# A third buffer for transposed q and k, a slot of lead for the heads' preparation, fewer score and half buffers

## The chip, the cores and the metric

The kernel runs on one core of one Trainium2 chip. The metric is the device time of one execution in microseconds (us). Engines are PE (TensorE, with its weight loads as PEld), DVE (VectorE), ACT (ScalarE), POOL (GpSimd) and SP (SyncE, which here only issues DMAs).

## The reference

Three layers follow each other on 4 x 576 = 2304 tokens, all in float32: causal attention with a decay (8 heads of 64), a gated two-branch layer, and a mixture of eight experts in which each token goes to one.

```python
scores = scale * np.matmul(q, k.transpose(0, 1, 3, 2))
cum = np.cumsum(np.log(np.clip(f, 0.0001, 1.0)), axis=-1)
scores = np.where(causal, -1000000000.0, scores + cum[:, :, :, None] - cum[:, :, None, :])
attn = np.exp(scores - scores.max(-1)); attn /= attn.sum(-1) + 1e-09
x = (attn @ v)                      # to (2304, 512)
g = x @ w_gate
x = (g * sigmoid(g) * (x @ w_val)) @ w_out
expert_idx = argmax(x @ r_gate)     # gate_w = softmax at that expert
out[mask] = gate_w * (relu(x[mask] @ w1[e]) @ w2[e])
```

## The kernel before, in words

Attention runs over 16 pairs of heads (4 batches, `NP` = 4 pairs each). A pair `P` takes four slots; slot `i` is head `hh` and group `g` of query rows in the order (0,0), (1,0), (0,1), (1,1). `slot(i)` issues the scores of item `i` (`part1`), the softmax halves of item `i-1` (`part2`) and the product with v of item `i-2` (`pv`), and beside them a piece of the next pair's preparation.

What a pair needs beforehand: `scales(P)` squares q and k on ACT (L189, into a junk tile `jk`), sums over partitions on PE (`tot`, L776) and makes scales on DVE. `prep(P, hh)` splits one head's q and k into f16 halves (`qks`: ACT L224 and L229, DVE L228) and transposes them by one DMA from SP (L231) into `qkt`, which `score` reads (L256, L257). `prep_v` does the halves of v (L242, L243). `v_scale(b)` loads a batch of v again in four pieces `vr` (L800) into buffers of the score pool and squares them on ACT (L801).

A score tile `st` of the pool `s` is written by DVE with the running maximum (L311), goes through the exponential on ACT (L321), and is split into f16 halves in a tile `p16` (name `p` in the trace) by DVE (L343) and POOL (L346, L357). One DMA from SP (L360) transposes `p16` into `pt`, whose products with v (L381) give `px`; from there `xn` (L394) and the next layer's input `xr`.

The next layer runs over 9 groups of 256 tokens, 6 units each (54 units): `g` and `v` (L491, 24 matmuls each) and `yp` (L544, 12). Its weights arrive as 8-byte floats and are decoded on ACT, DVE and POOL (L849 to L891) by a list of tasks, two of which (`PRE0`) come first and 43 (`PRE`) by the time the first 18 slots are issued. Then units and slots alternate. At the end come the experts (L1177, L1220).

The order on each engine is made by a scheduler out of the order in which the code issues, the buffers of the pools and its own estimate of times; an engine, and SP's queue, then work strictly in that order.

Of the kernel before, what the change touches and what calls it, by code (L numbers as in the profile page):

```python
# [7 lines left out]
F32 = mybir.dt.float32  # L8
F32R = mybir.dt.float32r
F16 = mybir.dt.float16  # L10
# [4 lines left out]
ACTF = mybir.ActivationFunctionType  # L15
# [12 lines left out]
def kernel(  # L28
# [15 lines left out]
    B, H, S, D = q.shape  # L44
# [7 lines left out]
    NCH = 5  # L52
# [93 lines left out]

    at = ExitStack()
    ap_ = at.enter_context(tc.tile_pool(name="att", bufs=1))
    NQK, NV, NPB, NBLK = 3, 1, 4, 9
    qk_in = [ap_.tile([128, 2, NCH, D], F32, name=f"qk_in{i}") for i in range(NQK)]  # L150
    v_in = [ap_.tile([128, 2, NCH, D], F32, name=f"v_in{i}") for i in range(NV)]
    p16s = [ap_.tile([128, NBLK, 128], F16, name=f"p16_{i}") for i in range(NPB)]
    qks_p = at.enter_context(tc.tile_pool(name="qks", bufs=2))
    qkt_p = at.enter_context(tc.tile_pool(name="qkt", bufs=2))
    vs_p = at.enter_context(tc.tile_pool(name="vs", bufs=2))
    s_p = at.enter_context(tc.tile_pool(name="s", bufs=5))
    st_p = at.enter_context(tc.tile_pool(name="st", bufs=4))
    xn_p = at.enter_context(tc.tile_pool(name="xn", bufs=1))
    xs_p = at.enter_context(tc.tile_pool(name="xs", bufs=1))
# [14 lines left out]
    def load_qk(P, a):  # L174
        if P < NPAIR:
            load_heads(qk_in[(2 * P + a) % NQK], (q, k)[a], P // NP, 2 * (P % NP))
# [7 lines left out]

    def scales(P):
        am = st_p.tile([128, 2], F32, tag="am", bufs=2, name="am")
        jk = qks_p.tile([128, 3 * NCH, 2, D], F16, tag="qks", name="jk").rearrange("p (a c) h d -> p a c h d", a=3)
        for a in range(2):
            act.activation(  # L189
                out=jk[:, a].rearrange("p c h d -> p h c d"), in_=qk_in[(2 * P + a) % NQK], func=ACTF.Square,  # L190
                accum_out=am[:, a:a + 1],
            )
        sc = st_p.tile([128, 2, 2], F32, tag="sc", name="sc")
        pow2_scale(sc[:, 0, :], sc[:, 1, :], [am])
        c = st_p.tile([128, 3], F32, tag="c", name="c")
        for i, (w, f_) in enumerate(((1, 0.125), (0, 8.0), (1, -0.125))):
            vec.scalar_tensor_tensor(
                out=c[:, i:i + 1], in0=sc[:, w, 0:1], scalar=f_, in1=sc[:, w, 1:2], op0=ALU.mult, op1=ALU.mult
            )
        nc_ = st_p.tile([128, 2, 128], BF16, tag="nc", bufs=2, name="nc")  # L200
        h0 = P // NP * H + 2 * (P % NP)
        act.activation(
            out=nc_, in_=pick[:, h0:h0 + 2].rearrange("p (h o) -> p h o", o=1).to_broadcast([128, 2, 128]),
            func=ACTF.Copy, scale=c[:, 1:2],
        )
        stt[P] = (sc, (c, nc_))
# [3 lines left out]
    def prep(P, hh):  # L210
        sc, c = stt[P]
        qks = qks_p.tile([128, 3 * NCH, 2, D], F16, tag="qks", name="qks")
        flat = qks.rearrange("p c h d -> p (c h d)")
        w = 2 * NCH * D

        def part(o, step, n):
            dims = [list(flat.ap[0])] + ([[step, n]] if n > 1 else []) + [[2 * D, NCH], [1, D]]
            return type(flat)(flat.tensor, flat.offset + o, dims)

        for a, n in ((0, 1), (1, 2)):  # L220
            src = qk_in[(2 * P + a) % NQK][:, hh]
            s1 = sc[:, 0, a:a + 1]
            hi, lo = [qks[:, NCH * a:NCH * a + NCH, x, :] for x in range(2)]
            act.activation(  # L224
                out=part(w, w + D, 2) if n > 1 else hi, func=ACTF.Copy, scale=s1,
                in_=src.rearrange("p (o c) d -> p o c d", o=1).to_broadcast([128, 2, NCH, D]) if n > 1 else src,
            )
            vec.scalar_tensor_tensor(out=lo, in0=src, scalar=s1, in1=hi, op0=ALU.mult, op1=ALU.subtract)  # L228
        act.activation(out=qks[:, 2 * NCH:, 0, :], in_=lo, func=ACTF.Copy)  # L229
        qkt = qkt_p.tile([128, 3, NCH * 128], F16, tag="qkt", name="qkt")  # L230
        sp.dma_start_transpose(out=qkt.rearrange("p a (c t) -> p (a c) t", t=128), in_=flat)  # L231
        heads[P, hh] = (qkt, c[1][:, hh, :])
# [3 lines left out]
    def prep_v(P):  # L236
        i = P % NV
        sb_ = sv[:, 0, P // NP:P // NP + 1]
        vs = vs_p.tile([128, 2, NCH, 2, D], F16, tag="vs", name="vs")
        for hh in range(2):  # L240
            src = v_in[i][:, hh]
            act.activation(out=vs[:, hh, :, 0, :], in_=src, func=ACTF.Copy, scale=sb_)  # L242
            vec.scalar_tensor_tensor(  # L243
                out=vs[:, hh, :, 1, :], in0=src, scalar=sb_, in1=vs[:, hh, :, 0, :], op0=ALU.mult, op1=ALU.subtract
            )
        vsp[P] = vs
# [193 lines left out]
    def slot(i):  # L440
        P = i // 4
        r = i % 4
        if i < NI:
            part1(i)
        if 0 <= i - 1 < NI:
            part2(i - 1)
        if 0 <= i - 2 < NI:
            pv(i - 2)
        if i % (4 * NP) == 10 and P // NP + 1 < B:
            v_scale(P // NP + 1)  # L450
        if P + 1 < NPAIR:
            if r == 0:
                scales(P + 1)
            if r == 1:
                prep_v(P + 1)
                if P + 2 < NPAIR:
                    load_v(P + 2)
            if r == 2:
                prep(P + 1, 0)
            if r == 3:  # L460
                prep(P + 1, 1)
                load_qk(P + 2, 1)
                load_qk(P + 3, 0)
# [280 lines left out]
    def start():  # L744
        consts()
        for t in qk_in:
            vec.memset(t[0:64, :, 0, :], 0.0)
        load_qk(0, 0)
        load_qk(0, 1)
        load_qk(1, 0)  # L750
        load_v(0)
        fs = s_p.tile([128, 576], F32, tag="s", name="fs")[0:B * H, 0:S]
        act.dma_start(out=fs, in_=f.rearrange("b h s -> (b h) s"))
        vec.tensor_scalar(out=fs, in0=fs, scalar1=1e-4, scalar2=1.0, op0=ALU.max, op1=ALU.min)
        act.activation(out=fs, in_=fs, func=ACTF.Ln)
        fz = s_p.tile([128, 576], F32, tag="s", name="fz")[0:B * H, 0:S]
        vec.tensor_tensor_scan(out=fz, data0=fs, data1=fs, initial=0.0, op0=ALU.add, op1=ALU.bypass)
        for i in range(3):
            hi = c_p.tile([128, S], BF16, tag="c", name="cumhi")[0:B * H]
            vec.tensor_copy(out=hi, in_=fz)  # L760
            vec.tensor_copy(out=cum3[B * H * i:B * H * i + B * H, :], in_=fz)
            if i < 2:
                vec.tensor_tensor(out=fz, in0=fz, in1=hi, op=ALU.subtract)
        fill = c_p.tile([128, NSLOT // 128], I32, tag="c", name="fill")
        gp.memset(fill, NT)
        act.dma_start(out=id_d.rearrange("(p a) o -> p (a o)", p=128), in_=fill)
        zr = c_p.tile([128, 512], F32, tag="c", name="zr")[0:1, :]
        gp.memset(zr, 0.0)
        act.dma_start(out=y_d[NT:NT + 1, :], in_=zr)
        act.dma_start(out=g_d[NT:NT + 1, :], in_=zr[:, 0:1])  # L770
# [24 lines left out]
    def v_scale(b):  # L795
        sq = st_p.tile([128, 4], F32, tag="sq", bufs=1, name="sq")
        n = VB // 4
        for i in range(4):
            t = s_p.tile([128, 576], F32, tag="s", name="vr")[:, 0:n]
            sp.dma_start(out=t, in_=vflat[b, :, i * n:(i + 1) * n])  # L800
            act.activation(out=t, in_=t, func=ACTF.Square, accum_out=sq[:, i:i + 1])  # L801
        pow2_scale(sv[:, 0, b:b + 1], sv[:, 1, b:b + 1], [sq[:, i:i + 1] for i in range(4)])
# [104 lines left out]
    def upto(n):  # L907
        while done[0] < min(n, len(tasks)):
            tasks[done[0]]()
            done[0] += 1  # L910
# [3 lines left out]
    def slots(n):  # L914
        while nslot[0] < min(n, NSL):
            slot(nslot[0])
            nslot[0] += 1
# [186 lines left out]
                    )), EP["xs"]))  # L1104

    PRE0, PRE = 2, 43
    start()
    upto(PRE0)
    scales(0)
    v_scale(0)  # L1110
    prep(0, 0)
    prep(0, 1)
    load_qk(1, 1)
    load_qk(2, 0)
    prep_v(0)
    load_v(1)
    first = 4 * NP + 2
# [199 lines left out]
    for s in range(NE + 1):  # L1317
        nxt = s + 1 if s < NE else None
        if s == 2:
# [9 lines left out]
                out=gwo, out_offset=None, in_=g_d[:, :],  # L1329
# [9 lines left out]
        if s < NE:  # L1339
            h = ht_p.tile([128, KF2, 2 * CAP], F32R, tag="h", name="h")  # L1340
# [29 lines left out]
    with tc.tile_pool(name="lw", bufs=1) as lw, tc.tile_pool(name="lr", bufs=3) as lr, tc.tile_pool(  # L1370
        name="lx", bufs=1
    ) as lx, tc.tile_pool(name="lp", bufs=2, space=PSUM) as lp:
        with tc.For_i(1, n_ov) as it:
# [4 lines left out]
            def lbank(tag):  # L1378
# [4 lines left out]
                out=gwl, out_offset=None, in_=g_d[:, :],  # L1383
# [4 lines left out]
            for src, n, nm in ((w1, KD, "a"), (w2, KF2, "b")):  # L1388
# [4 lines left out]
                for c in range(0, n, step):  # L1393
                    t = lr.tile([128, step, cols], F32, tag="r", name="r")
                    sp.dma_start(
                        out=t,
                        in_=src[bass.ds(e_i, 1), 128 * c:128 * (c + step), :].rearrange(
                            "o (k p) c -> p (o k) c", p=128
                        ),
# [39 lines left out]
```

## Time and profile before

| | us |
|---|---|
| median of 3 runs | 1037.69 (1036.25 to 1039.74) |
| the profiled execution | 1036.55 |
| its span | 1034.8 |
| busy in the span: PE, DVE, ACT, POOL | 885.4, 632.2, 558.0, 397.6 |

The median is 1.14 above the profiled execution, and 1.75 of that one's time lie outside its span. Busy time is an average over stages: the first stage has little for PE, the middle alternates units and slots, the last third has no attention.

### The profile page before, as it was taken

How to read it: one execution, taken by the hardware profiler on the slowest of the kernel's cores; microseconds unless marked ns; L12 is line 12 of the kernel's file. 1: busy time of each engine (PE TensorE's matmuls, PEld its weight loads, DVE VectorE, ACT ScalarE, POOL GpSimd, SP SyncE). 2: the span in 40 equal slices, each digit the busy share in tenths (PEclk: the TensorE clock that was granted, in tenths of full speed). 3: DMA queues.
4: the chain of work that ended last, by engine and by line, in shares of the span. 5: the costliest groups of instructions: out<-in, count | busy, mean ns of one | idle time of the engine just before them, and what ended most of it. 6: DMA issues, size and time to landing. Idle time of an engine off the chain costs nothing.

```text
span 1034.8 us, 19815 instructions
## 1 busy us (share of the span) xinstructions
PE 885.4 (86%) x7003; PEld 738.0 (71%) x7029; DVE 632.2 (61%) x1829; ACT 558.0 (54%) x1208; POOL 397.6 (38%) x473
## 2 busy tenths in 40 slices
PE   1545557989889988899899999999789899999995
PEld 0333436867667776788688878888668799899894
DVE  6999879497577575567765443234326787656440
ACT  5987988476576565556554231213225455555441
POOL 1567767364255234344444222222225643111101
PEclk9995557999999998999999999999898899999998
DMA  8897997258776768566754440203329987754430
GB/s 241 201 225 209 227 193 167 85 131 156 139 154 142 168 113 161 115 110 150 105 109 108 113 123 2 41 2 83 51 35 219 273 239 214 207 170 152 149 104 33
DMA packets 314409, 145.30 MB, mean 140 GB/s; under 512 B 279649, under 2 KB 292065, under 8 KB 314308
## 3 DMA queue, kind: packets, MB, share of 16 engines
q1 hardware_dynamic: 310016, 133.63, 55.7%
q0 software_dynamic: 4096, 10.24, 3.9%
q8 instruction: 56, 0.92, 0.4%
q14 instruction: 45, 0.37, 0.2%
q10 hardware_dynamic: 196, 0.14, 0.1%
HBM read 81.62 MB, written 10.31 MB: 89 GB/s over the span
## 4 chain that ended last, share of the span: by engine, by line
PE 42%; DMA 7%; issue 6%; ACT 3%; DVE 2%; POOL 2%; SPq 1%; POOLq 0%; DVEq 0%; ACTq 0%
PE bank L1220 9%; PE bank L1177 8%; PE yp L544 8%; PE v L491 7%; PE g L491 6%; DMA pair<-yt 1%; DMA out_dram<-o,ix 1%; POOL xg L1051 1%; PE px L381 1%; DMA qkt<-qks 1%; DMA pt<-p 1%; DMA pair<-words 1%; ACT st L321 1%; DMA wr<-in_moe_w_dram 1%; DVE st L311 1%
## 5 line engine op out<-in xcount | busy, mean ns | idle before, releaser
L491 PE MATMUL v<-xr,wv 128*128 128x256 f16 x1296 | 162.4, 281 | 0.0
L491 PE MATMUL g<-xr,wg 128*128 128x256 f16 x1296 | 161.4, 278 | 0.5 <-DMA xr<-xs 0.5
L491 PEld LDWEIGHTS <-wg 128*128 128x128 f16 x1296 | 123.6, 100 | 26.8 <-issue 9.2
L491 PEld LDWEIGHTS <-wv 128*128 128x128 f16 x1296 | 128.9, 101 | 18.9 <-issue 1.0
L346 POOL TENSOR_TENSOR p<-st,p 128x128 f16<-128x128 f32 (+3 forms) x128 | 108.7, 854 | 79.1 <-issue 52.4
L531 POOL TENSOR_TENSOR lo<-t,hi 128x512 fp32r<-128x512 f32 x54 | 71.5, 1324 | 148.6 <-ACT hi L530 123.4
L321 ACT ACTIVATE st<-st,nb,c 128x64 f32<-128x64 f32 (+4 forms) x160 | 102.6, 643 | 1.2
L381 PE MATMUL px<-vs,pt 128*128 128x64 f16 x1280 | 58.7, 203 | 41.0 <-DMA pt<-p 30.0
L343 DVE CAST p<-st 128x64 f16<-128x64 f32 (+4 forms) x160 | 71.8, 464 | 30.7 <-ACT st L321 21.9
L381 PEld LDWEIGHTS <-pt 128*128 128x128 f16 x1280 | 52.4, 106 | 52.4 <-DMA pt<-p 35.1
L514 ACT ACTIVATE t<-g,gscale 128x512 f32<-128x512 f32 (+3 forms) x72 | 39.3, 571 | 75.5 <-PE g L491 75.5
L256 PE MATMUL ps<-qkt 128*128 128x64 f16 (+2 forms) x192 | 56.7, 311 | 25.9 <-DMA qkt<-qks 11.3
L357 POOL TENSOR_TENSOR p<-st,p 128x64 f16<-128x64 f32 (+1 forms) x128 | 54.2, 425 | 61.5 <-DVE p L343 30.6
L1220 PE MATMUL bank<-whi,h 128*128 128x512 f32 x200 | 66.9, 400 | 4.8 <-ACT h L1182 4.8
L983 POOL DMA_INDIRECT out_dram<-o,ix x24 | 26.6, 1110 | 113.8 <-ACT o L1222 71.2
L311 DVE CUSTOM_DVE_ANT_0 st<-ps,zero 128x64 f32<-128x64 f32 (+3 forms) x160 | 55.6, 376 | 24.2 <-PE ps L264 21.0
L517 DVE SCALAR_TENSOR_TENSOR t<-t,g 128x512 f32<-128x512 f32 x54 | 36.9, 684 | 54.3 <-ACT t L514 54.2
L530 ACT ACTIVATE hi<-t 128x512 fp32r<-128x512 f32 x54 | 33.8, 625 | 60.8 <-DVE t L524 60.8
L949 DVE TENSOR_TENSOR wlo<-wr,whi 128x1024 fp32r<-128x1024 f32 x48 | 57.7, 1245 | 14.1 <-ACT whi L948 12.3
L257 PE MATMUL ps<-qkt 128*128 128x64 f16 (+2 forms) x192 | 59.9, 315 | 0.0
L544 PE MATMUL yp<-wohi,hi 128*128 128x512 f32 x144 | 59.7, 414 | 0.0
L1177 PE MATMUL bank<-xh,whi 128*128 128x320 f32 (+1 forms) x192 | 58.9, 309 | 0.5 <-ACT xh L93 0.5
(300 smaller groups left out, 2274.2 us busy)
## 6 DMA issues: line engine op xcount, KB each, us to landing
wr<-in_moe_w_dram SPq DMA_DIRECT2D x72, 512.0 KB
vr<-in_v_dram SPq DMA_DIRECT2D x16, 288.0 KB
qk_in<-in_q_dram SPq DMA_DIRECT2D x32, 128.0 KB
qk_in<-in_k_dram SPq DMA_DIRECT2D x32, 128.0 KB
v_in<-in_v_dram SPq DMA_DIRECT2D x32, 128.0 KB
y_d<-ys SPq DMA_DIRECT2D x6, 512.0 KB
wg<-in_moe_w_gate_dram SPq DMA_DIRECT2D x5, 512.0 KB
raw<-in_moe_w_val_dram SPq DMA_DIRECT2D x5, 512.0 KB
```

The lines of the kernel that those rows point to most:

```text
L257: pe.matmul(out=ps[:, o:o + n], lhsT=lq, rhs=qkt[:, 2, k0:k1], start=False, stop=False, skip_group_check=True)
L311: vec.tensor_tensor_reduce(out=sts[m][:, k0 - 64:k1 - 64], in0=ps[:, o:o + n], in1=zero.to_broadcast([128, n]), scale=1.0, scalar=init, op ...
L321: act.activation(out=sts[m], in_=sts[m], func=ACTF.Exp, scale=c[:, 0:1], bias=nb[:, m:m + 1], accum_out=sm[:, m, hh:hh + 1],)
L343: vec.tensor_copy(out=flat[:, o + 64:o + 64 + n], in_=src)
L346: gp.tensor_tensor(out=flat[:, o1:o1 + n - 64], in0=src[:, 64:n], in1=flat[:, o + 128:o + 64 + n], op=ALU.subtract)
L381: pe.matmul(out=px[:, 128 * m + 64 * hh:128 * m + 64 * hh + 64], lhsT=pm[:, o + ph * last + c, :], rhs=vs[:, hh, c, vh, :], start=(c == 0 ...
L491: pe.matmul(out=ps[:, fi, :], lhsT=w16[:, j, kk, wi, 128 * fi:128 * fi + 128], rhs=xr[:, kk, x0:x0 + 2, xi, :], start=(n_ == 0), stop=(n_ ...
L531: last["lo"] = gp.tensor_tensor(out=lo, in0=t, in1=hi.bitcast(F32), op=ALU.subtract)
L544: pe.matmul(out=yps[g][i], lhsT=hx[:, fi, 128 * i:128 * i + 128], rhs=wo[fk][wx], start=(j == 0 and n_ == 0), stop=(j == KF // 2 - 1 and n ...
L949: (eng or vec).tensor_tensor(out=l_, in0=t, in1=h_.bitcast(F32), op=ALU.subtract)
L1177: pe.matmul(out=p, lhsT=w[wi][:, kk, 128 * fk:128 * fk + 128], rhs=x[xi][:, kk, c0:CAP], start=(n_ == 0), stop=(n_ == 3 * KD - 1),)
L1220: pe.matmul(out=p[0:m, :], lhsT=hx, rhs=wx, start=(n_ == 0), stop=(n_ == len(prods) - 1))
```

## The change

It gives `qkt` a third buffer and pays for it with one score tile (`s`, 5 to 4) and one `p16` (4 to 3). The junk tile of `scales` is taken from `xn` (one buffer, else used by `pv`) instead of from `qks` (two buffers), once for q and once for k. `prep(P + 1, 0)` is issued in the second slot of a pair rather than the third, and `prep_v` in the third. At the start, the preparation of pair 0 comes ahead of the two weight tasks and of `v_scale(0)` and is marked as of high priority.

```diff
-    NQK, NV, NPB, NBLK = 3, 1, 4, 9
+    NQK, NV, NPB, NBLK = 3, 1, 3, 9
-    qkt_p = at.enter_context(tc.tile_pool(name="qkt", bufs=2))
+    qkt_p = at.enter_context(tc.tile_pool(name="qkt", bufs=3))
-    s_p = at.enter_context(tc.tile_pool(name="s", bufs=5))
+    s_p = at.enter_context(tc.tile_pool(name="s", bufs=4))
...
-        jk = qks_p.tile([128, 3 * NCH, 2, D], F16, tag="qks", name="jk").rearrange("p (a c) h d -> p a c h d", a=3)
         for a in range(2):
+            jk = xn_p.tile([128, 384], F32, tag="xn", name="jk").bitcast(F16)[:, 0:2 * NCH * D]
             act.activation(
-                out=jk[:, a].rearrange("p c h d -> p h c d"), in_=qk_in[(2 * P + a) % NQK], func=ACTF.Square,
+                out=jk.rearrange("p (h c d) -> p h c d", h=2, c=NCH), in_=qk_in[(2 * P + a) % NQK], func=ACTF.Square,
...
             if r == 1:
+                prep(P + 1, 0)
+            if r == 2:
                 prep_v(P + 1)
                 if P + 2 < NPAIR:
                     load_v(P + 2)
-            if r == 2:
-                prep(P + 1, 0)
...
-    start()
-    upto(PRE0)
-    scales(0)
-    v_scale(0)
-    prep(0, 0)
-    prep(0, 1)
+    with tc.high_priority():
+        start()
+        scales(0)
+        prep(0, 0)
+        prep(0, 1)
     load_qk(1, 1)
     load_qk(2, 0)
+    v_scale(0)
+    upto(PRE0)
     prep_v(0)
```

On SP at the start of the program, before; `qk_in_98`, `qk_in_99` and `qk_in_100` are the buffers of q and k, the first two those of pair 0:

```order
L168 DMA qk_in_99<-in_k_dram 64x2x64
L170 DMA qk_in_99<-in_k_dram 128x4x64 x2
L168 DMA qk_in_100<-in_q_dram 64x2x64
L170 DMA qk_in_100<-in_q_dram 128x4x64 x2
L168 DMA v_in_101<-in_v_dram 64x2x64
L170 DMA v_in_101<-in_v_dram 128x4x64 x2
L181 DMA v_in_101<-in_v_dram 64x2x64
L832 DMA raw<-in_moe_w_gate_dram 128x4x256
L832 DMA wg_92<-in_moe_w_gate_dram 128x4x256
L800 DMA vr<-in_v_dram 128x576 x4
```

The same place of the change:

```order
L168 DMA qk_in_99<-in_k_dram 64x2x64
L170 DMA qk_in_99<-in_k_dram 128x4x64
L800 DMA vr<-in_v_dram 128x576 x3
L170 DMA qk_in_99<-in_k_dram 128x4x64
L168 DMA qk_in_100<-in_q_dram 64x2x64
L170 DMA qk_in_100<-in_q_dram 128x4x64
L800 DMA vr<-in_v_dram 128x576
L170 DMA qk_in_100<-in_q_dram 128x4x64
```

Three of the four `vr` loads now stand ahead of the second half of pair 0's k, and all four ahead of the first weights.

On ACT at the same place, before, from the second square of pair 0 to the halves of its first head:

```order
L189 ACTIVATE jk,am<-qk_in_99 128x2x5x64
L766 DMA id_d<-fill 128x128
L769 DMA y_d<-zr 1x512
L770 DMA g_d<-zr 1x1
L849 ACTIVATE c<-raw 128x512
L202 ACTIVATE nc<-pick,c 128x256
L224 ACTIVATE qks<-qk_in_98,sc 128x5x64
```

And of the change, from the first square of pair 0 on:

```order
L189 ACTIVATE jk,am<-qk_in_98 128x640
L801 ACTIVATE vr,sq<-vr 128x576 x3
L766 DMA id_d<-fill 128x128
L769 DMA y_d<-zr 1x512
L770 DMA g_d<-zr 1x1
L801 ACTIVATE vr,sq<-vr 128x576
L189 ACTIVATE jk,am<-qk_in_99 128x640
L189 ACTIVATE jk,am<-qk_in_100 128x640
L224 ACTIVATE qks<-qk_in_98,sc 128x5x64
```

The decoding of weights (`c<-raw`) no longer stands between the squares and the halves; the four squares of `vr` and one of pair 1 do.

On SP later, where the first head of pair 9 is transposed (the only row of L231), before; the rows of L360 are the transposes of `p16`, with the buffer in the name:

```order
L360 DMA_TRANSPOSE pt<-p_1_103 128x9x128
L170 DMA qk_in_100<-in_q_dram 128x4x64 x2
L360 DMA_TRANSPOSE pt<-p_2_104 128x7x128
L168 DMA qk_in_98<-in_k_dram 64x2x64
L231 DMA_TRANSPOSE qkt<-qks 128x15x128
L412 DMA_TRANSPOSE xr<-xs 128x2x64
L417 DMA_TRANSPOSE xr<-xs 128x4x128
L360 DMA_TRANSPOSE pt<-p_3_105 128x9x128
L360 DMA_TRANSPOSE pt<-p_0_102 128x9x128
```

And of the change:

```order
L412 DMA_TRANSPOSE xr<-xs 128x2x64
L417 DMA_TRANSPOSE xr<-xs 128x4x128
L170 DMA qk_in_100<-in_q_dram 128x4x64 x2
L360 DMA_TRANSPOSE pt<-p_1_103 128x7x128
L360 DMA_TRANSPOSE pt<-p_2_104 128x9x128
L360 DMA_TRANSPOSE pt<-p_0_102 128x9x128
L231 DMA_TRANSPOSE qkt<-qks 128x15x128
```

Counted from the start of the program, this transpose stands behind 47 transposes of `p16` before, and behind 49 in the change.

## Rows read from the trace of the kernel before

**Rows 1.** Windows by stage: each engine's busy time, PE's granted clock, DMA share.

```profile
core 0: us, PE busy (x) PEld busy (x) DVE busy (x) ACT busy (x) POOL busy (x), PEclk, DMA share, GB/s
0.00:40.00 40.00, 13.23 (x64) 9.30 (x66) 28.77 (x103) 29.08 (x64) 12.11 (x23) 1.00 0.84 228
40.00:168.00 128.00, 67.20 (x597) 49.23 (x600) 115.94 (x314) 111.48 (x279) 85.98 (x95) 0.68 0.91 211
168.00:430.00 262.00, 235.51 (x2255) 191.25 (x2265) 175.79 (x565) 164.36 (x410) 121.17 (x160) 0.97 0.67 138
430.00:590.00 160.00, 154.17 (x1498) 127.07 (x1506) 98.71 (x366) 82.53 (x206) 67.12 (x92) 0.98 0.58 115
590.00:740.00 150.00, 148.37 (x1136) 124.44 (x1134) 53.66 (x173) 39.99 (x65) 32.76 (x29) 1.00 0.25 49
```

**Rows 2.** Waits of PE, 168 to 430 us: total us, times, longest.

```profile
PE px L381 <- DMA pt<-p: 8.0, 9, 1.6
PE tot L776 <- ACT vr L801: 7.7, 3, 3.9
...
PE ps L256 <- DVE xs L410: 2.0, 1, 2.0
...
PE ps L256 <- DMA qkt<-qks: 1.7, 1, 1.7
PE tot L776 <- ACT jk L189: 0.6, 1, 0.6
```

**Rows 3.** Timeline of ACT, start: start, length, in brackets idle before.

```profile
7.22 0.74 ACT L189 ACTIVATE jk<-qk_in 128x640 f16<-128x640 f32 x1 [1.52 <-DMA qk_in<-in_k_dram]
...
14.01 0.66 ACT L849 ACTIVATE c<-raw 128x512 f32<-128x512 f32 x1 [5.96 <-DMA raw<-in_moe_w_gate_dram]
...
14.97 2.44 ACT L224 ACTIVATE qks<-qk_in,sc 128x320 f16<-128x320 f32 x4
...
18.42 0.67 ACT L801 ACTIVATE vr<-vr 128x576 f32<-128x576 f32 x1
18.99 0.18 ACT L801 ACTIVATION_READ_ACCUMULATOR vr<-vr 128x1 f32 x1
```

**Rows 4.** Timeline of DVE, start.

```profile
14.70 0.43 DVE L851 TENSOR_SCALAR c<-c 128x512 int32<-128x512 int32 x1 [4.14 <-ACT c L849]
...
23.11 0.17 DVE L780 TENSOR_SCALAR tot<-tot 128x1 int32<-128x1 int32 x1 [2.72 <-PE tot L776]
```

**Rows 5.** Timeline of SP, start.

```profile
3.94 1.15 SPq L170 DMA_DIRECT2D qk_in<-in_k_dram  x2
...
10.64 3.69 SPq L800 DMA_DIRECT2D vr<-in_v_dram  x4
```

**Rows 6.** Timeline of PE, 217 to 320 us.

```profile
217.98 1.80 PE L491 MATMUL g<-xr,wg 128*128 128x256 f16 x15
...
300.13 0.20 PE L256 MATMUL ps<-qkt 128*128 128x64 f16 x1 [2.00 <-DVE xs L410]
...
318.10 0.20 PE L256 MATMUL ps<-qkt 128*128 128x64 f16 x1 [1.70 <-DMA qkt<-qks]
...
319.91 3.33 PE L491 MATMUL g<-xr,wg 128*128 128x256 f16 x15 [0.47 <-DMA xr<-xs]
```

**Rows 7.** Timeline of SP, 290 to 320 us.

```profile
295.89 1.98 SPq L231 DMA_TRANSPOSE qkt<-qks  x1
...
314.48 1.52 SPq L231 DMA_TRANSPOSE qkt<-qks  x1
```

**Rows 8.** Tile jk: idle time ahead of its instructions, us, times; timeline of ACT.

```profile
DMA qkt<-qks: 13.8, 8
...
300.17 0.74 ACT L189 ACTIVATE jk<-qk_in 128x640 f16<-128x640 f32 x1 [2.48 <-DMA qkt<-qks]
```

**Rows 9.** Waits of DVE, 168 to 430 us.

```profile
DVE p L343 <- DMA pt<-p: 6.8, 5, 4.7
```

**Rows 10.** SP's own waits, 168 to 430 us.

```profile
SPq L231 <- PE ps L264: 9.3, 2, 8.9
SPq L231 <- PE v L491: 9.0, 1, 9.0
```

## The prediction

> **What bounds the kernel now.** I read the windows by stage first. They show three regimes [rows 1]. Up to 168 us, DVE and ACT bound: from 40 to 168 us DVE is busy 115.94 of 128 us and ACT 111.48, while PE has 67.20 at a granted clock of 0.68 and waits. From 168 to 430 us PE bounds with holes, 235.51 of 262 us at 0.97. From 430 to 590 us it has 154.17 of 160, and from 590 to 740 us 148.37 of 150. So a stall that the change removes is worth something in the second stage, up to its 26.5 us of idle PE, and in the first only if it lets DVE or ACT do their work earlier. After 430 us PE's order is the same in both kernels, and a gain or loss that has reached PE by then is simply carried to the end.
>
> Second, the waits of PE in the second stage [rows 2]. The longest sums are for the transposed halves (`px` on `pt`, 8.0 us in 9 waits) and for the squares of v (`tot` on `vr`, 7.7 in 3). The transposed q and k that the third buffer is about cost 1.7 in one wait, and by the timeline a second one: at 300.13 a score waits 2.00, put down to `xs` on DVE [rows 6], but the transpose of pair 8's first head is issued on SP at 295.89 and takes 1.98 us there to issue [rows 7], and it is what the score reads; I count this one as a wait for `qkt` too. The junk tile costs PE 0.6 [rows 2].
>
> Third, the start. ACT begins the halves of pair 0 at 14.97 us, after an idle time of 5.96 us that ended with the first raw weights and after the decoding at 14.01 [rows 3]. DVE has idle times of 4.14 and 2.72 us there [rows 4].
>
> **The change part by part.**
>
> **The start.** Pair 0's halves no longer stand behind the weight decoding on ACT. But four squares of `vr` now do stand ahead of them, and on SP three `vr` loads are issued ahead of the second half of pair 0's k. Four such issues take 3.69 us, 0.92 each [rows 5], so the last part of k may be issued three times that, 2.8 us, later; the loads of k and q themselves take 1.15 us for two. So the loss is bounded at +2.8. The gain is bounded by what DVE idles there for the weights and the v scales, 4.14 + 2.72 = 6.9 us, since DVE's work in the first stage stays the same. No row is nearer to one end, so I take the middle, -2.0. As DVE is what bounds to 168 us, a gain that only brings PE's first scores forward and leaves DVE as idle as before would be worth nothing; I ask whether its idle time shrinks. The Trainium skill (Perfetto Trace Analysis, Identifying the Most-Contended Engine) puts it as a rule: improve the engine with the highest occupancy, and for the vector engine occupancy is a fair measure. The rows agree that this is DVE. Taken strictly, it would set this term to 0, and the sum below would come out 2.0 higher; I keep the middle, since two of DVE's idle times end with exactly the things that are moved.
>
> The rest of the first stage: the same tasks stand in another order on DVE and ACT, more weights early, more attention in the middle. DVE idles 128 - 115.94 = 12.06 us there [rows 1]. That is the most the new order can give; I let the loss reach as far, and take 0, since no row tells a side.
>
> **The third `qkt` buffer and the earlier `prep`.** It removes SP's wait for a buffer: 9.3 us before one head's transposes and 9.0 before another's [rows 10], with the transposes of `p16` queued behind. On the path are the two score waits, 2.00 and 1.70, and what follows the second: 15 matmuls of `g` take 3.33 us there against 1.80 at another place [rows 6], 1.53 more, a factor of 1.85, near the 2 between PE's two clock levels (an estimate; the rows have the granted clock only as a mean, 0.97 for the stage). Together 5.2 us. But the gain asks that the transposes move forward. In SP's order the first head of pair 9 stands behind 49 transposes of `p16` where 47 stood ahead before, and that of pair 8 behind 43 as before. So SP may still come to them as late: bounds -5.2 and 0, and I take half, -2.6.
>
> **The junk tile.** It no longer takes a `qks` buffer, whose release was by the transpose into `qkt`: ACT's squares waited 13.8 us in 8 waits for it, 2.48 of it at 300.17 [rows 8]. Only 0.6 of this reached PE [rows 2]: -0.6. It now shares one buffer with the output of `pv`; ACT idles enough (164.36 busy of 262) to cover a wait there, and if that cover is gone it costs a wait of the kind it replaces, 13.8/8 = 1.7 us.
>
> **Four score tiles, three of `p16`.** The scores of pairs 5 to 9 stand later in PE's order among the units, while `pv` stands where it did; so the work between a score and its `pv` (maximum, exponential, halves, transpose) has less time. PE's waits for this are 8.0 us in 9 waits, 0.9 each [rows 2]. I take two more, +1.8; bounds 0 and a doubling, +8.0. For `p16`, DVE already waits 6.8 us in 5 for a transpose to free a tile with four of them [rows 9]. With three I take one more such wait, 6.8/5 = +1.4, if DVE's lateness goes through to PE; bounds 0 (DVE is busy only 175.79 of 262 us in this stage, which hides it) and again a doubling, +6.8.
>
> **The squares of v.** The four `vr` pieces now fill the whole score pool. PE waits 7.7 us for them, 3.9 at the longest [rows 2]. With less room they may come later by one such wait, +3.9, or the whole may vanish since the order of the scales moves, -7.7. Taken: 0.
>
> **Sum.** -2.0 - 2.6 - 0.6 + 1.8 + 1.4 = -2.0, from the profiled execution's own 1036.55 to 1034.55. The median of the runs shown is 1.14 above that execution, so 1035.7.
>
> **The rivals.**
>
> *Faster.* The third buffer and the start both do all they can: -6.9 - 5.2 - 0.6 = -12.7, with nothing lost to the pools; 1023.9, or 1025.0 by the median. For it speaks that DVE's two idle times at the start end with moved work. Against it, that the transposes don't stand earlier in SP's queue, and that four `vr` issues now stand among the loads of k and q.
>
> *Slower.* Fewer buffers for scores and halves shorten the lead from a score to its `pv`. PE works in order, so it stands at `pv` for `pt` while units behind it could run. The wait of 8.0 us [rows 2] doubles, and the matmuls after each wait run at the slower level, as the 15 that lost 1.53 us [rows 6]: from +8 to +15 us, 1045 to 1052, and I take +10 with the small gains kept, 1047. Pairs 4 to 9 have 36 transposes of `p16` (six a pair); it decides as slower once each comes more than 3.1/36 = 0.09 us later at PE. That DVE waits for `p16` even with four speaks for it [rows 9]; against it, that PE's idle time in this stage is spread over several causes, and that the wait comes only 9 times. The Trainium skill (Perfetto Trace Analysis, Optimization Strategy) says that a gap that repeats on the engine that should be saturated can mean that there are too few buffers; the trace shows such gaps at `px`, nine of them, and no run here shows yet that buffers are their cause.
>
> *No change.* The third buffer stands there, but the transposes don't come earlier (49 and 47, 43 and 43), DVE's work at the start is only rearranged, and the pools are large enough: 1037 by the median.
>
> **How the numbers follow.** About 0.3% (3.1 us) is what a measurement of this kernel can tell from no change. The cases and their chances: the forecast, a small gain with its own range of 1032 to 1038.5, has 0.42 (0.13 faster by more than that, 0.27 within, 0.02 slower); the faster rival, with what lies between it and the forecast, 0.20; the slower rival 0.26; no change 0.12 (0.02, 0.09 and 0.01). So faster 0.13 + 0.20 + 0.02 = 0.35, within 0.27 + 0.09 = 0.36, slower 0.02 + 0.26 + 0.01 = 0.29. The range reaches to the faster rival, 1025, and over the lower part of the slower one, which spans 1045 to 1052, to 1048; about 0.1 is left out on each side.
>
> **What would show it.** The start: DVE's idle times of 4.14 and 2.72 us are shorter, and the first halves on ACT begin before 14.97 us, though the time at which PE's second stage begins (168 us) tells more. The third buffer: SP's waits for it of 9.3 and 9.0 us go, and the two score waits with them; if SP shows no such wait and PE still waits for `qkt`, the step is wrong. The junk tile: ACT's 13.8 us at `jk` go. The pools: PE's wait of `px` on `pt` between 168 and 430 us is near 10 us; over 15 means the slower rival. The prediction is wrong if the first stage comes out more than some 5 us longer or shorter, since there I set a whole stage's reordering at nothing, or if PE's idle time in the second stage moves by more than the terms above.

## The result and the profile after

The changed kernel takes 1058.78 us (median of 4 runs, 1052.9 to 1059.1) where the one before took 1038.72 (4 runs beside it). The ratio of the comparable runs is 1.0145, 95% interval 1.0101 to 1.0189: slower by 10 to 20 us (the medians are 20 apart, and one of the four runs of the kernel before took 1048.52). The profiled execution took 1059.07, with a span of 1057.2, 22.4 longer than before; that is more than the interval's upper end, so a part of what is taken apart below belongs to these two executions alone.

The windows by stage of the changed kernel, with columns as in [rows 1]; the first stage is cut once more at 184 us:

```profile
core 0: us, PE busy (x) PEld busy (x) DVE busy (x) ACT busy (x) POOL busy (x), PEclk, DMA share, GB/s
0.00:40.00 40.00, 12.52 (x67) 9.04 (x68) 29.86 (x103) 30.55 (x66) 12.26 (x23) 1.00 0.89 239
40.00:168.00 128.00, 58.97 (x479) 41.07 (x482) 108.19 (x279) 104.15 (x259) 84.30 (x88) 0.57 0.83 200
168.00:184.00 16.00, 12.06 (x121) 10.50 (x122) 11.32 (x43) 10.05 (x25) 4.35 (x8) 0.59 0.63 122
184.00:446.00 262.00, 234.69 (x2244) 189.54 (x2254) 165.06 (x558) 161.66 (x406) 115.60 (x157) 0.96 0.69 135
446.00:606.00 160.00, 151.21 (x1499) 125.32 (x1506) 101.15 (x366) 82.92 (x205) 67.61 (x93) 0.99 0.54 110
606.00:756.00 150.00, 148.22 (x1118) 123.92 (x1116) 53.36 (x174) 39.51 (x64) 32.86 (x28) 0.99 0.23 51
```

PE has done 479 matmuls from 40 to 168 us where it had done 597 [rows 1]; 16 us later it is level (667 against 661 up to 168). The last `g` and `v` matmul of the first unit (unit 0) ends at 184.4 us, at 168.5 before. So 16 of the 22 us are lost in the first stage. After it PE's busy time is near that of before in windows that start 16 us later: 234.69 against 235.51, 151.21 against 154.17, 148.22 against 148.37. The lag itself doesn't stay there: at the ends of the units it lies between 11.9 and 22.3 us, is 16.1 at unit 30 and grows from there to 22.4 at the end of the span.

Up to the end of the first unit DVE, the busiest engine of that stage, was busy 28.77 + 115.94 = 144.7 of 168 us before, and 29.86 + 108.19 + 11.32 = 149.4 of 184 after. Its idle time went from 23.3 to 34.6 us, +11.3, and its busy time rose by 4.7. That the two add up to the 16 is arithmetic and would hold for any engine. Up to 128 us the changed kernel's DVE idles 20.0 us where it idled 17.2, and from there to the end of the first unit 14.6 where it idled 6.1; so 8.5 of the 11.3 lie late in the stage. The windows from 128 us on, before:

```profile
128.00:168.50 40.50, 23.92 (x211) 17.48 (x209) 34.39 (x94) 35.01 (x84) 25.23 (x27) 0.57 0.95 194
```

and after:

```profile
128.00:184.40 56.40, 36.19 (x317) 27.56 (x318) 41.77 (x144) 43.00 (x110) 28.30 (x38) 0.62 0.80 180
```

What ended DVE's idle time up to the end of the first unit (total us, times, longest) includes waits for a score tile to come free (L311) and, after, for a `p16` (L343). Before, the only one of the kind:

```profile
DVE st L311 <- POOL p L357: 1.5, 2, 1.3
```

and after:

```profile
DVE p L343 <- DMA pt<-p: 4.4, 3, 2.5
...
DVE st L311 <- POOL p L357: 3.0, 5, 1.1
DVE st L311 <- ACT vr L801: 2.0, 1, 2.0
```

So 7.9 of the 11.3 us more of idle DVE ended with the release of a buffer of which the change has one fewer.

A hole of the new order, earlier in the stage, is seen on PE, the timeline of the changed kernel from 90 to 111 us (start, length, in brackets idle before):

```profile
90.93 0.31 PE L264 MATMUL ps<-maskgt,negid 128*128 128x128 bf16 x1
99.17 0.98 PE L381 MATMUL px<-vs,pt 128*128 128x64 f16 x15 [7.93 <-DMA pt<-p]
102.28 0.90 PE L423 MATMUL px<-ident,xn 128*128 128x128 f32 x3 [2.13 <-DVE xn L394]
107.17 0.37 PE L491 MATMUL g<-xr,wg 128*128 128x256 f16 x1 [3.98 <-ACT xr L434]
...
110.57 0.21 PE L256 MATMUL ps<-qkt 128*128 128x64 f16 x1
```

and on the others at the same time:

```profile
91.69 7.75 SPq L360 DMA_TRANSPOSE pt<-p  x3
...
92.42 0.69 DVE L852 SCALAR_TENSOR_TENSOR wo<-wg,wo 128x512 int32<-128x512 int32 x1
...
93.38 0.66 ACT L849 ACTIVATE wo<-wv 128x512 f32<-128x512 f32 x1 [2.04 <-DMA wv<-in_moe_w_out_dram]
...
94.07 0.43 DVE L851 TENSOR_SCALAR wo<-wo 128x512 int32<-128x512 int32 x1 [0.96 <-ACT wo L849]
...
94.69 1.69 POOL L855 TENSOR_TENSOR wo<-wo,wg 128x512 f32<-128x512 f32 x1 [2.13 <-ACT wg L850]
...
97.59 1.07 DVE L851 TENSOR_SCALAR wo<-wo 128x512 int32<-128x512 int32 x1 [2.36 <-ACT wo L849]
...
99.30 1.50 DVE L851 TENSOR_SCALAR wo<-wo 128x512 int32<-128x512 int32 x1
```

No score is issued from 91 to 110.6 us. PE stands in order at `pv`, whose three transposes take 7.75 us on SP, then at `xn` and at a unit that needs `xr`; meanwhile DVE, ACT and POOL decode weights, each waiting for the one before it in that chain and for a load. DVE itself idles only 0.96 + 2.36 us of it up to 99.30. That the decoding used up here is what is missing later, where DVE idles more, is argued, not shown. In the changed kernel's order on DVE 70 rows of it (L849 to L891) stand ahead of the last cast of the third pair, in the one before 52; from 168 to 184 us DVE, ACT and POOL are busy 11.32, 10.05 and 4.35 of 16.

The start of the changed kernel, timeline of ACT:

```profile
12.19 0.68 ACT L801 ACTIVATE vr<-vr 128x576 f32<-128x576 f32 x1 [1.81 <-DMA vr<-in_v_dram]
...
14.95 2.45 ACT L224 ACTIVATE qks<-qk_in,sc 128x320 f16<-128x320 f32 x4 [0.41 <-DVE sc L786]
```

that of DVE:

```profile
14.36 0.17 DVE L780 TENSOR_SCALAR tot<-tot 128x2 int32<-128x2 int32 x1 [4.52 <-PE tot L776]
```

and of SP, where the loads of v stand between the two halves of k:

```profile
3.93 0.60 SPq L170 DMA_DIRECT2D qk_in<-in_k_dram  x1
4.58 1.46 SPq L800 DMA_DIRECT2D vr<-in_v_dram  x3
6.09 0.43 SPq L170 DMA_DIRECT2D qk_in<-in_k_dram  x1
```

The halves of pair 0 begin at 14.95 us, at 14.97 before [rows 3]; the squares of v and their loads took the place of the weight decoding. DVE's idle time of 4.14 [rows 4] is one of 4.52; the one of 2.72 is gone, and up to 40 us DVE is busy 29.86 us in place of 28.77.

The second stage, waits of PE from 184 to 446 us (total us, times, longest), against [rows 2]:

```profile
PE px L381 <- DMA pt<-p: 13.7, 13, 4.7
PE ps L256 <- DVE mx L311: 5.9, 1, 5.9
PE tot L776 <- ACT vr L801: 3.1, 2, 2.0
PE ps L256 <- DMA qkt<-qks: 1.5, 1, 1.5
...
PE tot L776 <- ACT jk L189: 0.2, 1, 0.2
```

In the same stretch, DVE's wait for a free `p16`, against [rows 9]:

```profile
DVE p L343 <- DMA pt<-p: 13.5, 8, 2.5
```

and SP's longest wait before a transpose of q and k, against [rows 10]:

```profile
SPq L231 <- PE yp L544: 8.7, 1, 8.7
```

### The profile page after: what moved, and what is told of

Read it like the earlier page. It is cut to its first block, busy times and chain, and to the rows that moved or that the text cites. A ratio compares the mean times of both kernels' runs of the same rounds, so it can differ in the third digit from the quotient of the medians.

```text
span 1057.2 us, 19850 instructions
## 1 busy us (share of the span) xinstructions
PE 887.5 (84%) x7005; PEld 738.7 (70%) x7029; DVE 627.6 (59%) x1829; ACT 560.2 (53%) x1208; POOL 393.4 (37%) x473
## 5 line engine op out<-in xcount | busy, mean ns | idle before, releaser
L491 PEld LDWEIGHTS <-wv 128*128 128x128 f16 x1296 | 126.7, 100 | 28.1 <-issue 12.4
L381 PE MATMUL px<-vs,pt 128*128 128x64 f16 x1280 | 61.2, 206 | 43.6 <-DMA pt<-p 32.6
L343 DVE CAST p<-st 128x64 f16<-128x64 f32 (+4 forms) x160 | 64.4, 423 | 41.1 <-ACT st L321 21.6
L311 DVE CUSTOM_DVE_ANT_0 st<-ps,zero 128x64 f32<-128x64 f32 (+3 forms) x160 | 56.3, 376 | 21.0 <-PE ps L264 15.0
L949 DVE TENSOR_TENSOR wlo<-wr,whi 128x1024 fp32r<-128x1024 f32 x48 | 57.6, 1244 | 15.7 <-ACT whi L948 15.1
```

The lines of the kernel that those rows point to most:

```text
L343: vec.tensor_copy(out=flat[:, o + 64:o + 64 + n], in_=src)
L381: pe.matmul(out=px[:, 128 * m + 64 * hh:128 * m + 64 * hh + 64], lhsT=pm[:, o + ph * last + c, :], rhs=vs[:, hh, c, vh, :], start=(c == 0 ...
L491: pe.matmul(out=ps[:, fi, :], lhsT=w16[:, j, kk, wi, 128 * fi:128 * fi + 128], rhs=xr[:, kk, x0:x0 + 2, xi, :], start=(n_ == 0), stop=(n_ ...
L949: (eng or vec).tensor_tensor(out=l_, in0=t, in1=h_.bitcast(F32), op=ALU.subtract)
```

## The experiments

All ratios are to the kernel before, run on the same chip, with 95% intervals; "unit 0 at" gives the end of the first unit's last `g` or `v` matmul in the profile. The expectations give times; since the kernel before took 1032.2 to 1040.8 us on the chips of these runs, times and ranges compare only to some us, and the ratios come first. Theory A puts the loss on the new start, B on the smaller pools, C on the earlier preparation.

**The new start alone.** The edit is the last hunk of the diff above, on the kernel before.

> The kernel before with the new start alone (pair 0's preparation first and of high priority, the squares of v and the two weight tasks after it); buffers, junk tile and order of the preparation as before. Theory A (the new start brings more weight decoding forward and attention later in the first 168 us): 1053 to 1060 us, the first unit ends near 184 us. Theory B (too few score tiles and halves in the first stage): 1036 to 1040, the first unit near 168. Theory C (the preparation a slot earlier takes ACT and DVE from the pair that is running): as B, 1036 to 1040.

1.0066 (1.0043 to 1.0089), unit 0 at 175.9: between what A and what B and C gave.

**The start undone.** The changed kernel with before's start.

```
-    with tc.high_priority():
-        start()
...
+    start()
+    upto(PRE0)
+    scales(0)
+    v_scale(0)
```

> The changed kernel with the start of before. Theory A: the loss is gone, 1034 to 1040, first unit ends near 168 us. Theory B or C: the loss stays, 1053 to 1060, first unit near 184.

1.0159 (1.0129 to 1.0188), unit 0 at 179.1. The loss stays without the start: A falls as the cause of it.

**The pools alone.**

```
+    NQK, NV, NPB, NBLK = 3, 1, 3, 9
+    qkt_p = at.enter_context(tc.tile_pool(name="qkt", bufs=3))
+    s_p = at.enter_context(tc.tile_pool(name="s", bufs=4))
```

> The kernel before with the buffers of the change alone (three qkt, four score tiles, three p16). Theory B: 1050 to 1060, with more waits for p16 and score tiles on DVE and PE before 168 us. Theory A or C: 1035 to 1041.

1.0192 (1.0165 to 1.0218), unit 0 at 183.4: as B, and no less than the whole change (the intervals overlap). The waits that B named are there too: up to unit 0 DVE waits 4.4 us for a `p16` and 3.3 for a score tile, 0 and 1.5 before.

**The preparation's order alone.**

```
             if r == 1:
+                prep(P + 1, 0)
+            if r == 2:
                 prep_v(P + 1)
```

> The kernel before with the order of the preparation alone (first head's prep in the second slot, prep_v in the third); two qkt buffers. Theory C: 1050 to 1060. Theory A or B: 1035 to 1041, since without a third qkt buffer the transposes can't come earlier.

1.0083 (1.0054 to 1.0113), unit 0 at 181.1. Between the theories, as the start was. B was now taken apart.

**Four score tiles alone** (`bufs=5` to `4` in `s_p`).

> The kernel before with four score tiles, nothing else. If the score tiles carry the loss of pools_only (20.6 us there): 1048 to 1056, and the first unit ends near 184 us. If it is the p16 tiles: 1032 to 1037, as the kernel before. If the order that the scheduler makes changes with any edit and costs some 8 us each, as in start_only and order_only: 1039 to 1044.

1.0147 (1.0109 to 1.0184), unit 0 at 182.8: in the range for the score tiles as carriers of the loss.

**Three `p16` alone** (`NPB` 4 to 3).

> The kernel before with three p16, nothing else. If the p16 tiles carry the loss of pools_only: 1048 to 1056, with longer waits of the cast on DVE for a transpose to free a tile, before 168 us. If it is the score tiles: 1032 to 1037. If any edit costs some 8 us by the order: 1039 to 1044.

1.0146 (1.0117 to 1.0176), unit 0 at only 172.9; most of its loss comes in the second stage. The whole, 1047.17, is just under the range for the `p16` tiles as carriers, and the longer wait of the cast that it named is there (3.8 us up to unit 0, 0 before). So each of the two cuts alone loses what was expected of only one of them.

**Both cuts, two `qkt`.**

> The kernel before with four score tiles and three p16, but still two qkt. If the cuts are the cause and the third qkt buffer gives nothing back: 1050 to 1056, as pools_only. If the third buffer itself is what brings the transposes into the way: 1033 to 1042.

1.0181 (1.0155 to 1.0208), as `pools_only`: the third `qkt` buffer gives nothing back, and the cuts together cost hardly more than either.

**The junk tile alone** (the hunk of `scales`).

> The kernel before with the junk tile in the xn pool, nothing else. If the squares now wait on the one xn buffer, and the scales with them: 1037 to 1045. If the wait at qks that it ends was off the path: 1032 to 1036. If any edit costs some 8 us by the order: 1039 to 1044.

1.0167 (1.0130 to 1.0203), above all three ranges. A tile that touches neither `s` nor `p16` costs as much as these. The parts' losses alone add up to 0.66 + 0.83 + 1.92 + 1.67 = 5.1%, and all together make 1.45%. So they are not prices that add up. Theory D: each edit makes the scheduler find another order over the whole first stage, and the order of before is a good one.

**Two controls and two neighbours.** The only edit is `PRE`, here for 42:

```
-    PRE0, PRE = 2, 43
+    PRE0, PRE = 2, 42
```

> A control: the kernel before with PRE = 42 in place of 43, so that one weight task fewer is issued beside the first 18 slots; no buffer, tile or preparation is touched. Theory D (the order of before is an unusually good one, and any edit that makes the scheduler find another order loses about what the single parts lost, 8 to 18 us): 1040 to 1052. Theory E (each of the parts costs through its own resource, and the loss of all together saturates): 1029 to 1037, as the kernel before.

1.0076 (1.0047 to 1.0105).

> A second control: the kernel before with PRE = 44, one weight task more beside the first 18 slots, nothing else. Theory D: 1040 to 1052. Theory E: 1029 to 1037.

1.0040 (1.0021 to 1.0059).

> The changed kernel with PRE = 42. Theory D: the changed kernel is one draw among the orders with its buffers; a neighbour lies anywhere from 1040 to 1060, on average no higher than the neighbours of before by more than a few us. Theory E: 1050 to 1058 in every neighbour, some 15 to 20 above the neighbours of before.

1.0164 (1.0109 to 1.0218).

> The changed kernel with PRE = 44. Theory D: anywhere from 1040 to 1060. Theory E: 1050 to 1058.

1.0184 (1.0139 to 1.0230). One weight task more or less, with no buffer touched, costs 0.4 to 0.8%; the medians, 1041.79 and 1037.89, lie inside D's range and between those of D and E: D has a part. The neighbours of the change lie 10.5 and 13.8 us above those of before by the medians, more than D's few and less than E's 15 to 20. It was what the trace shows of the hole at 91 to 110 us that led to theory F, the place of the weight decoding, against G, the buffers themselves. The edit that moves the decoding, here later:

```
-        upto(PRE0 + (PRE - PRE0) * (i + 1) // first)
+        upto(PRE0 + int((PRE - PRE0) * ((i + 1) / first) ** 1.3))
```

**The change with the decoding later, by the powers 1.3 and 1.6.**

> The changed kernel with the weight tasks issued later among the first 18 slots (share of tasks by slot i is ((i+1)/18) to the power 1.3 in place of 1). In DVE's order 54 rows of weight decoding then stand ahead of the last cast of the third pair, where the changed kernel has 70 and the one before 52. Theory F (the decoding comes too early and is missing later): 1034 to 1042, and DVE idles less than 30 us before the end of the first unit. Theory G (the smaller buffers stall the chain whatever the order): 1046 to 1054, DVE's idle time stays near 34.

1.0107 (1.0073 to 1.0141). The window up to the end of unit 0 (173.6 us):

```profile
0.00:174.00 174.00, 79.96 (x668) 58.40 (x672) 146.65 (x415) 143.25 (x342) 102.33 (x118) 0.70 0.91 211
```

DVE idles 174 - 146.65 = 27.4 us in place of 34.6: of the 15.9 us that unit 0 came later, 10.8 are gone, with all small buffers kept. That is as F says. The whole is not: the median, 1053.83, lies in G's range, though on a chip where the kernel before took 1040.83; the interval of the ratio overlaps that of the change, and DVE still waits 7.4 us for score tiles and `p16` up to unit 0. By the end of the last unit its profile is 15.1 us behind before's, 10 of them lost after unit 0, among them these waits of PE from 168 to 430 us:

```profile
PE px L381 <- DMA pt<-p: 12.0, 14, 2.8
PE ps L256 <- DVE mx L311: 5.2, 1, 5.2
PE g L491 <- DVE t L517: 3.7, 1, 3.7
```

> The same with the power 1.6: 50 rows of weight decoding ahead of the last cast of the third pair on DVE. Theory F: 1032 to 1042. Theory G: 1046 to 1054.

1.0175 (1.0121 to 1.0229), unit 0 at 179.4, with 34.4 us of idle DVE, 13.0 of them waits for score tiles and `p16`: here moving the decoding back gave nothing in the whole. F misses.

**The kernel before with the decoding earlier** (power 0.7) **and later** (1.3).

> The kernel before with all its buffers and the weight tasks issued earlier (power 0.7): 62 rows of weight decoding ahead of the last cast of the third pair on DVE, and 48 in place of 38 ahead of that of the second. Theory F: 1045 to 1055, with DVE's idle time up from 23 us to over 30. Theory G: 1037 to 1043, what any new order costs.

1.0164 (1.0104 to 1.0224). Up to the end of unit 0, at 181.8:

```profile
0.00:182.00 182.00, 82.23 (x665) 59.67 (x670) 149.80 (x429) 147.63 (x358) 109.27 (x125) 0.68 0.88 205
```

32.2 us of idle DVE with every buffer in place, 0.8 of them waits for score tiles and none for `p16`: as F, and as much loss as the change itself.

> The kernel before with the weight tasks issued later (power 1.3): 54 rows ahead of the last cast of the third pair. Its decoding stands where it did, so theory F: 1033 to 1042, as the controls with PRE 42 and 44. Theory G: the same. If moving the decoding back is a gain by itself: below 1030.

1.0113 (1.0082 to 1.0144): outside the interval of F and of G. A kernel with all buffers and the decoding where it was can lose 1.1% too.

**Start and preparation order together.**

> The kernel before with the new start and the new order of the preparation together, all buffers and the junk tile as before. If each part has a price of its own (0.66% and 0.83% alone): 1.5% above the kernel before, some 16 us. If a loss comes with any new order, and not by part: 0.4 to 1.0%, as one part alone; 58 rows of weight decoding stand ahead of the last cast of the third pair on DVE, as in start_only.

1.0018 (0.9996 to 1.0041), below both ranges and no change that can be told, where each alone lost 0.66 and 0.83%. Up to unit 0's end, at 173.8:

```profile
0.00:174.00 174.00, 82.89 (x670) 59.90 (x670) 154.18 (x429) 147.31 (x357) 106.66 (x125) 0.67 0.93 215
```

DVE idles 19.8 us, less than before's 23.3, and is busy 9.5 us more by then; the last unit ends 2.4 us earlier than before's. So neither part has a fixed price. The kernel has as many rows of decoding early (58) as the start alone, so this count is not the whole measure.

**The junk tile with the decoding later.**

> The kernel before with the junk tile in the xn pool, as in junk_only (which had 64 rows of decoding ahead of the last cast of the third pair on DVE, and lost 1.67%), and the weight tasks issued later by the power 1.3 (48 rows). Theory F: the first unit ends before 177 us in place of 183, and the whole lies 0.3 to 1.1% above the kernel before. Theory G, the one xn buffer itself stalls the squares: 1.4 to 1.9% above, the first unit still near 183.

1.0067 (1.0041 to 1.0093), unit 0 at 167.9, where the junk tile alone had 1.0167 and 183.2. The windows up to there, of the junk tile alone and of this kernel:

```profile
0.00:183.00 183.00, 83.20 (x672) 61.17 (x673) 148.78 (x430) 146.94 (x356) 100.52 (x121) 0.67 0.89 204
```

```profile
0.00:168.00 168.00, 71.41 (x670) 52.87 (x671) 144.12 (x408) 138.56 (x336) 100.33 (x117) 0.74 0.91 213
```

Idle DVE 34.2 and 23.9 us: the same xn buffer with another order loses 0.7% in place of 1.7%. As F, and G falls for this part.

**What is settled.** The loss of the change is no sum of prices of its parts: they don't add up, a new order alone loses up to 1.6% with all buffers and hardly a wait for them (before_pow07), and with the small buffers kept the end of the first unit moves by 10.8 us when only the decoding is moved (after_pow13). That early decoding is what makes an order bad isn't shown: with 50 rows of it ahead of the last cast of the third pair unit 0 ends at 179.4 (after_pow16), with 58 at 172.9 to 175.9 (p3_only, start_order, start_only). A direct comparison of the buffers is had where the order doesn't differ: from unit 20 on PE's order of scores, `pv` and units is the same in the kernels with four score tiles, three `p16` and both as in before, and from the end of unit 20 to that of the last unit they take 326.6, 326.9 and 326.4 us, before 326.9. There the missing buffers show no cost, to within some us: kernels with all buffers and that same order took 327.2 to 327.7 there on two other chips, and 331.3 and 332.9 on a third.

**What stays open.** How much of the first stage is the order and how much the buffers. The ten kernels with fewer `s` or `p16` lose 1.60% on average (1.07 to 1.92), the seven with all buffers and the junk tile where it was, before itself left out, 0.80% (0.18 to 1.64). Up to the end of unit 0 DVE waits for score tiles and `p16` 8.2 us on average in the ten (4.6 to 13.0) and 3.1 in the seven (0.8 to 7.6), so the buffers may cost by these waits themselves; the ranges of both overlap. That fewer buffers make a bad order likelier, since the scheduler, which knows them, puts other work where attention can't go on, fits this too but isn't shown. The test would be one order with both buffer counts in the first stage, and it was not made, because the scheduler makes the order out of the buffers. PE's granted clock from 40 to 168 us was lower as well, 0.57 against 0.68, with PE busy less; what that adds to the chain of a pair was not taken apart. None of the 19 kernels was faster than before.

## Why the prediction was wrong

It gave 1035.7, a range from 1025 to 1048 and 0.29 for slower; the kernel is at 1058.78, with before at 1038.72 beside it. The step that failed: **"The rest of the first stage: the same tasks stand in another order ... and take 0, since no row tells a side."** Measured, +16 us: DVE's idle time +11.3, close to the bound of 12.06 that the text had named and then not used, and its busy time +4.7, where it had taken DVE's work in the first stage to stay the same. With it failed the place of the pools' price: the terms for four score tiles and three `p16` were worked out from waits after 168 us alone, while up to the end of the first unit DVE's waits for the two went from 1.5 to 9.4 us. Whether these waits or the order around them cost the 16 us stays open.

A second step failed, with less weight: "After 430 us PE's order is the same in both kernels, and a gain or loss that has reached PE by then is simply carried to the end." PE's order differs up to some 520 us of the kernel before (from 498.8 us on, 15 products with v stand elsewhere among the units), and behind that, from unit 30 on, the lag still grew from 16.1 to 22.4 us.

Term by term:

- *The start, -2.0:* -1.1 by DVE's idle time up to 40 us, none of it at the first halves: the four squares of `vr`, named as what might eat the gain, ate it there, 14.95 against 14.97 us. The whole stage gained nothing. The rule that the text had weighed there (Trainium skill, Perfetto Trace Analysis, Identifying the Most-Contended Engine), and by which earlier first scores are worth nothing unless DVE works more, would have set the term to 0; the traces agree with it in that DVE stayed the busiest engine of the stage, 149.4 of 184 us against 144.8 of ACT.
- *The third buffer, -2.6:* the waits for `qkt` in the second stage fell from 3.7 (with the one put down to `xs`) to 1.5, -2.2: right in size. SP's waits of 9.3 us went; in place of that of 9.0 stands one of 8.7.
- *The junk tile, -0.6:* 0.6 to 0.2 in the second stage, right, and ACT's squares no longer wait for `qkt`. The 13.8 us of that wait were of the whole program, 6.2 of them in this stage, and stood beside PE's 0.6 of the stage alone. That the move changes the first stage was not seen.
- *Four score tiles, +1.8:* `px` on `pt` 8.0 to 13.7, +5.7, inside the bounds of 0 and +8.0. But the runs don't give it to the pools: in the 262 us after unit 0 this wait is 3.5 us with four score tiles alone, 3.8 with three `p16` alone and 7.1 with both.
- *Three `p16`, +1.4:* DVE's wait for a free one 6.8 to 13.5, the doubling that stood as the upper bound; 7.3 with three `p16` alone. PE's part of it can't be told from the term before.
- *The squares of v, 0:* 7.7 to 3.1, -4.6, inside the bounds.
- *The second stage as a whole* was forecast at -2.6 - 0.6 + 1.8 + 1.4 = 0; PE's busy time in its 262 us fell by 0.8. That the sum fits is luck: +5.7 at `px` and 3.5 more (2.4 to 5.9) for scores behind the running maximum `mx`, in no term, against -4.6 for the squares of v, taken at 0, and -2.2.
- *What was not in the sum:* another 6.4 us between the end of the first stage and that of the span (866.8 before, 873.2 after). Nearly all of it comes after unit 30, where the lag grows by 6.3; one wait of PE there, for the experts' input `xg`, is 9.0 us in place of 6.7, and the rest was not taken apart.

The slower rival had the right side and the wrong place: PE does stand at `pv` for `pt`, and those waits grew by 5.7 us in the second stage without moving it, short of the 15 us that would have been its sign; the 16 us were lost in the first, where it had put nothing. The rule beside it (Trainium skill, Perfetto Trace Analysis, Optimization Strategy), that repeated gaps can mean too few buffers, is neither borne out nor refuted by the first stage, where DVE's waits for the cut buffers grew by 7.9 us while a kernel with all buffers lost as much; where the order is equal, the runs show no cost of fewer buffers.

The chances were put on the mechanisms of the diff. What was missing is a case for the order itself: that any edit lets a scheduler find another one, here 0.2 (no change that can be told) to 1.6% slower with no buffer taken away.

## What to carry to other kernels

Where a scheduler makes the order, run a control that changes nothing but the order (here one weight task more or less) before giving a part of a change a price; here such controls moved the time by 0.4 to 0.8%, more than any single term of the sum. Split the length of a stage, up to a mark that all versions reach, into idle and busy time of its busiest engine, and read what ended the idle time, by place and by buffer: here most of the growth lay late in the stage and ended with the release of a buffer that the change had cut, which waits read in another stage could not tell. The mark alone is not the whole: with start and preparation together unit 0 ended 5.3 us later and the run took no longer. Where filler work such as the decoding should stand is not settled: moved later, unit 0 ended earlier than without the move in three kernels and later in one, and only the one with the junk tile clearly lost less in the whole.

## What the runs showed of the hardware

The rise of DVE's busy time in the first stage was for the most part not more work, and instructions of one shape took unequal times. From 40 to 168 us both kernels run 24 instructions of L851 and 24 of L852 on DVE, in 35.2 us before and 40.7 after. Two of these groups before (busy us, mean ns of one):

```profile
L851 DVE TENSOR_SCALAR wo<-wo 128x512 int32<-128x512 int32 x16 | 8.8, 565 | 0.0
...
L852 DVE SCALAR_TENSOR_TENSOR wo<-wg,wo 128x512 int32<-128x512 int32 x8 | 6.9, 862 | 0.0
```

and after:

```profile
L851 DVE TENSOR_SCALAR wo<-wo 128x512 int32<-128x512 int32 x16 | 12.5, 780 | 6.2 <-ACT wo L849 6.2
...
L852 DVE SCALAR_TENSOR_TENSOR wo<-wg,wo 128x512 int32<-128x512 int32 x8 | 9.0, 1122 | 0.1
```

The same shape took 0.43 us at 94.07, with POOL idle, and 1.50 at 99.30, beside a POOL instruction:

```profile
98.71 1.80 POOL L891 TENSOR_TENSOR wolo<-wo,wohi 128x512 fp32r<-128x512 f32 x1 [0.33 <-ACT wohi L890]
```

Up to the end of the first unit of both kernels, the 25 of L851 that ran while POOL was idle took 0.39 to 0.43 us and the 24 of L852 0.68 to 0.69; the 69 of either that ran beside a POOL instruction took 0.41 to 1.78.

The Trainium skill (SBUF — State Buffer, SBUF: two separate sides) says that DVE and GpSimd share a port pair, and that a GpSimd instruction and a DVE instruction that needs the pair too (one in a mode that uses both ports, or, against a GpSimd instruction that reads SBUF, one with two inputs there) exclude each other: whichever starts first holds it for the whole instruction. The rows agree with it in that none of these was long without POOL. A run that keeps POOL away from these instructions was not made, so that this is the cause of the 5.5 us is argued, not shown. Other groups of DVE moved both ways: the 43 casts of L343 up to the end of the first unit took 23.4 us before and 17.9 after.
